# Eight quarter-sized casting weight loads for four halves, and a newly searched unit order, in a fused linear-attention and feed-forward kernel

## The chip, the cores and the metric

The kernel runs on one core of one Trainium2 chip. The metric is device time in microseconds (us). Every comparison below sets a kernel beside the kernel before, run in turn with it on the same chip in the same rounds. A ratio is the mean time of one kernel's fast runs over the mean of the other's fast runs of the same rounds, so it is not quite the ratio of the medians that are quoted; its 95% interval follows in brackets. For a single core a run counts as slow when it is over 1.5% above the fastest of the same kernel. Two changed kernels were mostly run in different rounds, so they are compared through their ratios to the kernel before. The time covers a little more than the profiled span: 195.0 us beside a span of 192.9 us in the profiled run of the kernel before.

## The reference, cut to what matters

```python
# q, k, v, alpha: (4 batches, 8 heads, 768 steps, 48), float32
for t in range(S):
    state = alpha[:, :, t, :, None] * state + einsum('bhd,bhe->bhde', k[:, :, t], v[:, :, t])
    y[:, :, t] = einsum('bhd,bhde->bhe', q[:, :, t], state)
x = y.transpose(0, 2, 1, 3).reshape(3072, 384)
h = x @ w_in                # (384, 2048)
out = (h * cos(h)) @ w_out  # (2048, 384)
```

## The kernel before

The sequence is cut into 24 chunks of 128 steps. Each chunk needs four loads (alpha, k, q, v, with rows of 192 bytes), the logarithm of alpha, cumulative sums on TensorE, exponentials, two scalings, transposes of q and k, scores, a state update and the attention output. Its output then goes through the two layers. All of it is written as small **units**, and one string gives their order; each engine runs its own units in that order. A unit waits for its inputs, and everything behind it on the same engine waits with it. So the order is the schedule.

```python
units = {
    "a": load_a, "k": load(k_t, k), "q": load(q_t, q), "v": load(v_t, v), "w": load_w,   # w from GpSimd, the rest on the SP queue
    "l": ..., "C": ..., "E": ...,        # logarithm (ScalarE), cumulative sums (TensorE), exponentials (ScalarE) of a pair of chunks
    "K": scale_k, "R": lambda j: scale_q(nc.gpsimd, j), "O": lambda j: scale_q(nc.vector, j),
    "P": cast_v, "M": decay,             # GpSimd
    "T": transposes, "t": ev_transposes, # on TensorE, copied out by VectorE
    "D": dma_transposes,                 # or as one DMA on the SP queue
    "S": state, "A": scores, "Q": outputs_two, ...
    "F"/"H": first layer, "f"/"h": Sin, "p"/"g": gate, "V": second layer (a quarter), "o": store, "x": warmup,
}
for u in ORDER.split():
    units[u[0]](int(u[1:]))

def load_w(i):                           # float32 in memory, bfloat16 on the chip: a casting DMA, issued by GpSimd
    n = NF // 2
    if i < 2:
        f = slice(i * n * C, (i + 1) * n * C)
        nc.gpsimd.dma_start(out=w1[:, :, f], in_=moe_w_in[:, f].rearrange("(k p) f -> p k f", p=C))
    else: ...                            # the halves of w_out

def dma_transposes(j):
    nc.sync.dma_start_transpose(qkT[j % 4]..., kqb[j % 4]...)
```

The loads, the stores and the DMA transposes share one queue, SP. A DMA transpose whose input is not ready holds every load behind it; in the trace of the kernel before, such waits add up to 20.6 us.

## Time and profile before

| | before |
|---|---|
| median of 3 runs | 195.2 us (195.06 to 195.44) |
| profiled span, granted clock | 192.9 us, 1.00 |
| busy: TensorE, VectorE, ScalarE, GpSimd | 95%, 61%, 62%, 42% |
| DMA row | 8 or 9 tenths from about 5 to 150 us |
| TensorE waits after 46 us | 1.8 us in all |

A busy share says how long an engine had work, not whether it was the bound. Here two rows are full, TensorE's and the DMA row, and TensorE's includes 17 us of warm-up matmuls that compute nothing. The chain of waits and the list of TensorE's waits tell more: TensorE waits for data until 43 us (the **ramp**) and is fed afterwards (the **rest**). The lines are in the prediction.

### The profile page before, as it was taken

Reading aid. Unit: us, or ns where it says so; the run is one execution under the profiler, and the core shown is the slowest. Engines: PE = TensorE matmul, PEld = TensorE weight load, DVE = VectorE, ACT = ScalarE, POOL = GpSimd, SP = SyncE. Lnnn points to the kernel's source line nnn. Section 1 sums busy time; section 2 is a strip of 40 time slices with the busy share of each in tenths; the row PEclk is TensorE's granted clock in tenths of the full one; section 3 lists DMA queues with packets and bytes.
Section 4 is the critical chain, followed back from the end, with each engine's and each line's share of the span. In section 5 each row is a group of like instructions: output and inputs, shape, how many; then the busy total and the mean of one; then the engine's idle time right before and its main releaser. Section 6 shows DMA issues by size and latency. Waiting matters only on the chain.

```text
span 192.9 us, 4781 instructions
## 1 busy us (share of the span) xinstructions
PE 182.5 (95%) x1990; PEld 131.8 (68%) x1994; DVE 117.7 (61%) x138; ACT 120.1 (62%) x133; POOL 81.6 (42%) x128
## 2 busy tenths in 40 slices
PE   7997889989999999997999998999999999999993
PEld 2444468957688687685777685786786786876861
DVE  5025784844847928829828438748758578596450
ACT  2540344744768668947739567789999982361632
POOL 3317950055294655571190656271239761030000
PEclk9999999999999999999999999999999999999999
DMA  6999999999989999999989999999998762200112
GB/s 127 188 187 188 146 190 188 184 196 194 190 192 176 205 233 207 188 168 196 268 162 192 175 214 218 175 227 205 149 217 158 135 152 34 85 0 3 41 41 82
DMA packets 123092, 31.23 MB, mean 162 GB/s; under 512 B 117184, under 2 KB 122304, under 8 KB 123072
## 3 DMA queue, kind: packets, MB, share of 16 engines
q1 hardware_dynamic: 120192, 27.80, 85.0%
q0 software_dynamic: 2880, 3.15, 10.1%
q8 instruction: 15, 0.25, 0.5%
q14 instruction: 5, 0.04, 0.1%
HBM read 25.17 MB, written 4.72 MB: 155 GB/s over the span
## 4 chain that ended last, share of the span: by engine, by line
PE 66%; DMA 13%; SPq 6%; ACT 4%; issue 4%; DVE 3%; POOL 2%; ACTq 0%; DVEq 0%
PE one L362 31%; PE two L341 21%; DMA w<-in_moe_w_out_dram 10%; PE two L303 6%; SPq L158 5%; PE two L243 3%; DVE g_sb L352 3%; DMA v_sb<-in_v_dram 2%; ACT c_sb L347 2%; PE two L191 2%; SPq L161 2%; ACT L347 1%; PE one L257 1%; POOL w L167 1%; PE two L193 1%
## 5 line engine op out<-in xcount | busy, mean ns | idle before, releaser
L352 DVE TENSOR_TENSOR g_sb<-two,c_sb 128x1024 bf16<-128x1024 f32 x48 | 58.0, 1221 | 27.7 <-ACT c_sb L347 27.2
L362 PE MATMUL one<-w,g_sb 128*128 128x384 bf16 x384 | 69.5, 327 | 1.4 <-DVE g_sb L352 0.8
L341 PE MATMUL two<-xT,w 128*128 128x256 bf16 (+1 forms) x624 | 68.4, 264 | 1.0 <-DVE g_sb L352 1.0
L347 ACT ACTIVATE c_sb<-two,halfpi 128x1024 bf16<-128x1024 f32 x48 | 52.6, 1113 | 19.5 <-PE two L341 19.0
L341 PEld LDWEIGHTS <-w 128*128 128x128 bf16 x624 | 56.7, 98 | 9.7 <-issue 1.1
L362 PEld LDWEIGHTS <-g_sb 128*128 128x128 bf16 x384 | 35.3, 98 | 24.0 <-DVE g_sb L352 1.7
L206 POOL TENSOR_TENSOR kqb<-k_sb,icp 128x384 bf16<-128x384 f32 x24 | 23.9, 997 | 20.5 <-DMA k_sb<-in_k_dram 12.6
L262 POOL TENSOR_TENSOR ub<-sc,Em 128x384 bf16<-128x384 f32 x20 | 16.6, 829 | 33.1 <-DVE sc L272 31.8
L248 DVE TENSOR_TENSOR A_sb<-two,mask_f 128x1024 bf16<-128x1024 f32 x24 | 28.5, 1217 | 2.6 <-PE two L243 2.6
L212 POOL TENSOR_TENSOR kqb<-q_sb,cp 128x384 bf16<-128x384 f32 x22 | 21.9, 998 | 9.4 <-DMA q_sb<-in_q_dram 5.7
L366 ACT ACTIVATE o_sb<-one 128x384 f32<-128x384 f32 x24 | 11.7, 492 | 15.5 <-PE one L362 15.5
L347 ACT ACT_TABLE_LOAD x11 | 14.1, 1283 | 9.9 <-PE two L341 6.2
L216 POOL CAST vpb<-v_sb 128x384 bf16<-128x384 f32 x24 | 12.0, 504 | 17.2 <-DMA v_sb<-in_v_dram 9.3
L375 PE MATMUL one<-warm 128*128 128x512 bf16 x62 | 17.1, 418 | 2.2 <-DVE warm L102 1.2
L185 ACT ACTIVATE lnab<-a_sb 128x768 bf16<-128x768 f32 (+1 forms) x13 | 10.3, 794 | 12.5 <-DMA a_sb<-in_alpha_dram 12.4
L201 ACT ACTIVATE icp<-two 128x768 f32<-128x768 f32 (+1 forms) x13 | 9.9, 761 | 11.8 <-PE two L193 9.0
L272 DVE TENSOR_TENSOR sc<-one,ub 128x384 f32<-128x384 f32 x20 | 11.0, 552 | 8.2 <-PE one L257 7.9
L321 DVE CAST xT<-two 128x768 bf16<-128x768 f32 x11 | 10.5, 958 | 8.4 <-PE two L303 8.4
L179 ACT ACT_TABLE_LOAD x11 | 14.1, 1283 | 0.9 <-PEq L404 0.7
L303 PE MATMUL two<-A_sb,vpb 128*64 128x128 bf16 x264 | 13.2, 220 | 0.1
L303 PEld LDWEIGHTS <-vpb 128*64 128x64 bf16 x288 | 12.8, 110 | 0.5 <-issue 0.3
L375 PEld LDWEIGHTS <-warm 128*128 128x128 bf16 x66 | 6.4, 104 | 9.6 <-issue 3.6
(42 smaller groups left out, 114.1 us busy)
## 6 DMA issues: line engine op xcount, KB each, us to landing
k_sb<-in_k_dram SPq DMA_DIRECT2D x24, 192.0 KB, 4.6
a_sb<-in_alpha_dram SPq DMA_DIRECT2D x24, 192.0 KB, 4.3
v_sb<-in_v_dram SPq DMA_DIRECT2D x24, 192.0 KB, 4.4
q_sb<-in_q_dram SPq DMA_DIRECT2D x24, 192.0 KB, 4.2
out_dram<-o_sb SPq DMA_DIRECT2D x24, 192.0 KB, 3.7
w<-in_moe_w_in_dram POOLq DMA_DIRECT2D x2, 768.0 KB, 10.0
w<-in_moe_w_out_dram POOLq DMA_DIRECT2D x2, 768.0 KB, 17.7
qkT<-kqb SPq DMA_TRANSPOSE x16, 3.8
```

What stands on the lines that cost most here:

```text
L179: nc.scalar.preload_act_table_set("natural_log_exp_and_others")
L206: nc.gpsimd.tensor_tensor(out=kqb[j % 4][:, 0, :, 0:D], in0=k_t[j % 6], in1=icp_t[j // 2 % 3][:, j % 2].rearrange("s (h d) -> s h d", h=H) ...
L212: eng.tensor_tensor(out=kqb[j % 4][:, 1, :, 0:D], in0=q_t[j % 6], in1=cp.rearrange("s (h d) -> s h d", h=H), op=ALU.mult)
L216: nc.gpsimd.tensor_copy(out=vpb[j % 4][:, :, 0:D], in_=v_t[j % 6])
L248: nc.vector.tensor_tensor(out=A_t[j % 4].rearrange("s (h t) -> s h t", h=H), in0=two[("A", j)].rearrange("s (h t) -> s h t", h=H), in1=mas ...
L262: eng.tensor_tensor(out=ub[j % 3][:, :, 0:96].rearrange("r p (a e) -> r p a e", a=2), in0=src.rearrange("r p (a e) -> r p a e", a=2), in1= ...
L303: nc.tensor.matmul(t[64 * half : 64 * half + 64, kt * C : (kt + 1) * C], lhsT, rhs, start=start, stop=stop, skip_group_check=True)
L341: nc.tensor.matmul(t[:, m * n : (m + 1) * n], w1[:, kk, f * C : (f + 1) * C], x_t[g % 3][:, kk, bs].rearrange("r b t -> r (b t)"), start=( ...
L347: nc.scalar.activation(out=c_s.take((name, i)), in_=two[(name, i)], func=AF.Sin, bias=halfpi, scale=1.0)
L352: nc.vector.tensor_tensor(out=g_t[g % 3][:, fs, bs], in0=shaped(two[(name, i)], name), in1=shaped(c_s[(name, i)], name), op=ALU.mult)
L362: nc.tensor.matmul(one[("o", j)][:, 0:DM], g_t[j // 2 % 3][:, f, j % 2], w2[:, f], start=(f == 0), stop=(f == NF - 1))
L375: nc.tensor.matmul((one.free or two.free)[0][:, 0:512], warm[:, 0:C], warm, start=True, stop=True)
```

## The change

Its intent: the weights are to come in smaller steps, so that the first layer waits for fewer of them at a time. The first unit F0 still needs both quarters of the first half of w_in, 768 KB (in bfloat16); only the later, smaller units H can do with 384 KB. The order of all units was searched anew, by a local search over a recalibrated timing model. In the new order eight more of the q and k scalings run on VectorE, chunks 5, 6 and 7 are transposed by DMA instead of TensorE, and the activation table is switched 20 times instead of 22.

```diff
 ORDER = """
-k1 a0 a3 a1 k0 v1 q0 a2 q2 i0 x12 c0 v3 d0 k2 M0 i1 x7 c1 k3 K0 d1 q1 K1 q3 P1 O0 x13 T0 v0 l1 t0
...
-C3 m4 b4 o2 V12 E3 m5 V13 k7 S5 Q2 l4 u5 M7 M6 o0 R6 C4 z2 a11 M5 K6 V14 E4 H10 v7 b5 q8 T6 P6 k8
-H8 t6 h10 R7 q11 S6 a10 V15 h8 g10 K7 H9 q9 e3 u6 g8 M9 T7 k9 M8 h9 H11 t7 k10 P7 g9 V16 h11 v8 R8
...
+a2 w1 a1 a0 a3 i0 l1 i1 v0 k0 q3 q0 k3 P0 x32 C1 c0 d0 B0 w0 x6 S0 R0 M0 c1 v1 d1 E1 x1 T0 t0 u0
...
+k6 q7 k7 e2 E3 V12 o0 q6 v6 V13 M6 R7 K7 K6 l4 m5 Q2 C4 z2 E4 S5 V14 H10 P6 H8 a11 v7 D7 P7 M7 h10
+O6 u5 H9 S6 V15 D6 g10 h8 H11 h9 e3 g8 u6 V16 S7 A7 g9 u7 h11 A6 V17 m7 a10 m6 o2 k8 q8 k9 a13 v9
... (27 lines each, all replaced)
@@ load_w @@
-        n = NF // 2
-        if i < 2:
+        n = NF // 4
+        if i < 4:
...
-            i -= 2
+            i -= 4
@@ scale_k takes the engine; "B" is new @@
-        "K": scale_k,
+        "K": lambda j: scale_k(nc.gpsimd, j), "B": lambda j: scale_k(nc.vector, j),
```

More of the change, by code (lines that the diff above doesn't have):

```diff
@@ L17 @@
 ORDER = """
-k1 a0 a3 a1 k0 v1 q0 a2 q2 i0 x12 c0 v3 d0 k2 M0 i1 x7 c1 k3 K0 d1 q1 K1 q3 P1 O0 x13 T0 v0 l1 t0
-a5 x2 C1 E1 a4 v2 K2 q5 R2 K3 k5 x15 T2 O1 t2 T1 k4 A0 t1 q4 P0 x1 A1 w0 S1 S0 a6 u0 w1 u1 l2 M1
-m0 R3 x8 C2 w2 m1 T3 E2 M2 Y0 w3 t3 A2 y0 P2 Y1 m2 b1 S2 A3 M3 P3 u2 M4 m3 b2 Q1 x6 F0 z1 y1 S3 f0
-F2 p0 f2 x2 F3 p2 F1 f3 H6 p3 f1 H4 p1 h6 u3 V4 h4 g6 b3 V5 V0 g4 V1 v4 H5 a7 V2 h5 v5 R5 V3 g5 V6
-a8 e0 K5 V7 a9 H7 K4 e1 q6 R4 T5 h7 V8 t5 k6 V9 g7 T4 v9 P4 V10 t4 v6 V11 l3 S4 e2 A4 q7 u4 A5 P5
@@ L23 @@
-C3 m4 b4 o2 V12 E3 m5 V13 k7 S5 Q2 l4 u5 M7 M6 o0 R6 C4 z2 a11 M5 K6 V14 E4 H10 v7 b5 q8 T6 P6 k8
-H8 t6 h10 R7 q11 S6 a10 V15 h8 g10 K7 H9 q9 e3 u6 g8 M9 T7 k9 M8 h9 H11 t7 k10 P7 g9 V16 h11 v8 R8
-S7 A6 u7 A7 o1 V17 m6 b7 V20 a13 m7 V21 V18 a12 l5 g11 Q3 o3 R9 C5 z3 v10 K8 V19 E5 H12 K9 D8 e4
-R11 H14 D9 M10 P8 H13 h12 K10 o4 q10 k11 g12 S8 h13 V22 v11 V23 u8 h14 q12 g13 H15 b8 e5 P10 k12
-g14 V28 M11 k13 h15 P9 S10 V29 a15 g15 V30 a14 A8 R10 l6 A9 m8 V31 v12 K11 C6 e7 m9 E6 S9 D10 P11
-Q4 u9 b9 D11 V24 z4 R12 V25 u10 v13 H18 K12 v14 b10 H16 D12 h18 H19 q15 g18 h16 o5 P12 S11 g16 h19
@@ L29 @@
-H17 M12 v15 u11 o7 V26 g19 h17 V27 a16 P13 V32 g17 e6 M13 A10 q13 A11 m10 S12 V33 o6 l7 V34 a17
-m11 C7 k14 Q5 E7 a18 u12 A12 z5 P15 V36 R15 V37 m12 K13 V38 H22 R13 M15 H20 D13 b11 h22 P14 H21
-q19 g22 K14 h20 q17 q14 V35 g20 v16 h21 V39 k15 q21 e8 H23 g21 e9 o9 V40 h23 S13 V41 u13 R14 g23
-A13 V44 b13 l8 D14 V45 m13 V46 K15 q20 V47 v17 C8 D15 Q6 E8 P16 q16 V42 z6 a19 e11 V43 M16 R17 k17
-H24 o8 q18 P17 k16 M14 S14 a21 h24 H25 u14 b14 e10 g24 S15 h25 o10 H26 R16 k18 g25 V48 h26 K17 H27
-u15 g26 D17 b15 V52 h27 V53 a20 K16 v18 A15 A14 a23 m15 V49 D16 l9 V50 m14 V54 v19 C9 g27 Q7 E9
@@ L35 @@
-K18 V55 z7 V51 R18 e13 H28 o13 e12 R19 a22 o12 S16 M18 D18 S17 u16 H30 h28 b16 o11 g28 H29 q23 P19
-h30 k19 P18 v22 M17 u17 V60 q22 h29 g30 V56 H31 g29 l10 A17 A16 m17 V61 V62 K19 m16 h31 V57 D19
-V58 g31 C10 k20 Q8 E10 V59 z8 V63 R20 e14 H32 o14 e15 b17 k21 o15 K20 S18 k23 S19 u18 H34 h32 v21
-R21 u19 D20 M19 g32 H33 b19 h34 v20 K21 v23 V68 g34 h33 k22 M20 V64 D21 H35 g33 P21 l11 A18 A19
-m18 V69 V70 P20 m19 M21 h35 V65 V66 g35 C11 Q9 E11 P22 V67 z9 P23 K23 V71 e16 H36 o16 e17 M22 R23
-o17 S20 R22 D23 H38 u20 h36 b20 H37 g36 h38 K22 M23 S21 D22 g38 h37 V76 H39 u21 g37 b21 V72 h39
@@ L41 @@
-A21 A20 m21 V77 V78 m20 V73 V74 g39 A22 Q10 V75 z10 V79 e18 m22 H40 o18 e19 o19 S23 h40 S22 H42
-u22 b22 g40 H41 h42 u23 V80 b23 g42 h41 H43 g41 A23 h43 V84 m23 V81 g43 V82 Q11 V83 z11 V85 e20
-H45 o20 V86 h45 H44 g45 H47 h44 H46 g44 h47 V87 g47 h46 V88 e21 V89 g46 o21 V92 V93 V90 V91 V94
-e22 V95 o22 e23 o23
+a2 w1 a1 a0 a3 i0 l1 i1 v0 k0 q3 q0 k3 P0 x32 C1 c0 d0 B0 w0 x6 S0 R0 M0 c1 v1 d1 E1 x1 T0 t0 u0
+B3 x3 A0 k1 m0 R3 M3 P1 M1 K1 M2 q1 x5 T3 a5 a4 t3 k2 Y0 y0 w3 x1 A3 q2 S1 F0 O1 l2 T1 C2 m3 u1 R2
@@ new lines @@
+E2 t1 B2 A1 m1 v2 x3 T2 t2 w2 w4 P2 b1 Y1 A2 y1 S2 v3 m2 F2 P3 f0 u2 b2 S3 p0 w5 w6 f2 Q1 k4 q5 k5
+p2 M4 w7 u3 z1 x1 F1 f1 F3 V4 V0 H5 f3 h5 p1 p3 g5 v4 q4 a6 a7 H6 H4 M5 b3 K5 V5 H7 K4 P4 h6 h4 h7
+V1 g6 g4 O5 V6 O4 g7 V7 V2 V3 e1 V8 e0 D5 V9 T4 t4 V10 V11 S4 a9 v5 a8 u4 o1 b4 l3 A4 m4 P5 A5 C3
+k6 q7 k7 e2 E3 V12 o0 q6 v6 V13 M6 R7 K7 K6 l4 m5 Q2 C4 z2 E4 S5 V14 H10 P6 H8 a11 v7 D7 P7 M7 h10
+O6 u5 H9 S6 V15 D6 g10 h8 H11 h9 e3 g8 u6 V16 S7 A7 g9 u7 h11 A6 V17 m7 a10 m6 o2 k8 q8 k9 a13 v9
+q9 v8 l5 V20 b5 V21 V18 C5 Q3 g11 V22 V19 z3 M8 B9 R8 M9 K8 R9 b7 P8 H12 H14 E5 h12 e4 H13 V23 g12
@@ new lines @@
+h14 g14 h13 e5 H15 g13 S8 V28 u8 o3 k11 a12 v10 h15 b8 P9 D9 D8 V29 A9 A8 V30 g15 m8 k10 q10 o5
+v11 k12 o4 q11 a14 k13 a16 m9 V31 l6 e7 C6 P10 K10 S9 S10 E6 u9 Q4 V24 O10 z4 V25 P11 b9 O11 u10
+K11 M10 M11 K12 b10 M12 H18 M13 K13 S11 H16 h18 h16 H19 g18 h19 H17 q12 D10 q13 u11 D11 R12 g16
+g19 h17 V26 a15 V27 e6 D12 o7 R13 V32 A11 A10 V36 l7 g17 k14 D13 v12 V37 V38 C7 V39 m11 m10 o6 b11
+k15 P12 a17 Q5 k17 v13 v14 q15 E7 q14 A12 A13 V33 z5 m12 m13 V34 H22 V35 H20 e9 l8 h22 e8 h20 P13
+K15 K14 P14 R15 R14 g22 S13 H21 S12 H23 h21 g20 u12 Q6 V44 g21 u13 z6 h23 C8 g23 a18 o9 v15 q17 o8
@@ new lines @@
+k16 k19 q16 a19 v16 D15 V45 H24 H25 S14 V46 E8 h24 b13 H26 V47 u14 g24 V40 h25 M14 M16 b14 R17 K17
+P15 g25 h26 e11 K16 V41 D14 A14 P16 g26 l9 M15 v17 A15 m14 m15 V42 V43 S15 C9 v18 q18 o11 k18 q19
+D17 Q7 e10 z7 u15 E9 H27 H30 S16 H28 P18 K18 R18 R16 a20 q21 o10 h27 V52 h28 D16 g27 b15 h30 R19
+a23 u16 g28 g30 V53 H29 V54 V48 V55 A16 A17 K19 b16 P17 M18 M17 k23 a21 k20 v20 v22 V49 V50 D19
+h29 g29 l10 e13 m17 m16 C10 V51 S17 Q8 z8 o13 H31 e12 E10 S18 H33 h31 u17 u18 g31 V56 V60 v21 o12
+D18 k22 a22 k21 v19 P21 P20 P19 K21 q22 q20 q23 h33 g33 A18 A19 V57 V58 H32 l11 h32 m18 m19 g32
@@ new lines @@
+V59 e14 Q9 V61 S19 C11 H34 V62 u19 z9 E11 h34 g34 V63 H35 H39 V64 e15 h35 h39 g35 g39 b17 H36 V65
+M19 K20 b19 R21 V66 R20 R22 R23 K22 P22 M20 K23 V67 o14 h36 e16 H38 S20 D21 D22 o15 g36 u20 h38
+M21 M22 b20 H37 S21 V68 V69 h37 V70 u21 D23 D20 g38 g37 V72 V71 A21 A20 A23 V73 e17 m20 m21 V74
+V75 Q10 m23 z10 A22 V76 e18 o16 S22 V77 H40 v23 V78 h40 V79 H41 e19 P23 M23 o17 b21 h41 m22 u22
+g40 b22 Q11 H42 S23 o18 z11 V84 H43 h42 h43 u23 g42 g41 g43 V80 H44 V81 V82 h44 H46 V85 V83 H45
+V86 e20 h46 h45 g44 V88 V87 e21 g45 g46 o19 o20 o21 H47 h47 V89 V92 g47 V90 V93 V94 V91 e22 o22
@@ L45 @@
+V95 e23 b23 o23
 """
@@ L203, in exps, with scale_k @@
         two.give(("c", j))
-    def scale_k(j):
-        nc.gpsimd.tensor_tensor(out=kqb[j % 4][:, 0, :, 0:D], in0=k_t[j % 6],
+    def scale_k(eng, j):
+        eng.tensor_tensor(out=kqb[j % 4][:, 0, :, 0:D], in0=k_t[j % 6],
                                 in1=icp_t[j // 2 % 3][:, j % 2].rearrange("s (h d) -> s h d", h=H),
@@ L379 @@
         "l": lambda g: ln(2 * g, 2), "C": lambda g: cums(2 * g, 2), "E": lambda g: exps(2 * g, 2),
-        "K": scale_k, "R": lambda j: scale_q(nc.gpsimd, j), "O": lambda j: scale_q(nc.vector, j),
+        "K": lambda j: scale_k(nc.gpsimd, j), "B": lambda j: scale_k(nc.vector, j), "R": lambda j: scale_q(nc.gpsimd, j), "O": lambda j: scale_q(nc.vector, j),
         "P": cast_v, "M": decay,
```

## The prediction

> **What bounds the kernel now.** I began with the page: its first part (engine shares) and the row of DMA busy tenths. TensorE's matmul row is busy nearly all the time, and the DMA row stands at 9 until about 155 us, so both are suspects and neither share says which one a change would move.
>
> ```profile
> PE 182.5 (95%) x1990; PEld 131.8 (68%) x1994; DVE 117.7 (61%) x138; ACT 120.1 (62%) x133; POOL 81.6 (42%) x128
> ...
> q0 software_dynamic: 2880, 3.15, 10.1%
> ```
>
> The 95% is not all work. The busy time by stretches, restricted to the warm-up line L375 (columns: stretch, its length, PE busy and count, PEld busy and count, clock, DMA share, GB/s), shows 17 us of dummy matmuls, all before 42.8 us:
>
> ```profile
> 0.00:28.50 28.50, 15.44 (x56) 5.88 (x60) 1.00 1.20 170
> 28.50:42.80 14.30, 1.62 (x6) 0.55 (x6) 1.00 1.25 194
> ```
>
> The waits of PE after 42.8 us are these three and no others, 2.3 us in all:
>
> ```profile
> PE two L341 <- DVE g_sb L352: 1.0, 1, 1.0
> PE one L362 <- DVE g_sb L352: 0.8, 1, 0.8
> PE one L362 <- DMA w<-in_moe_w_out_dram: 0.5, 1, 0.5
> ```
>
> So there are two regimes: a ramp of 43 us, in which TensorE waits or warms itself, and 147 us in which it is fed. The chain that ended last names what sets the ramp (start, length, what):
>
> ```profile
> 13.86 4.62 DMA v_sb<-in_v_dram
> ...
> 18.53 0.50 POOL vpb L216
> 19.04 1.65 POOL w L167 x2
> ...
> 22.92 19.84 DMA w<-in_moe_w_out_dram
> ...
> 42.80 2.76 PE one L362 x16
> ```
>
> The weight DMAs stand behind a cast of v in GpSimd's program order, so they are issued only at 19 to 23 us, and the last half lands at 42.76. The timeline of the SP queue shows what they do to the other loads meanwhile:
>
> ```profile
> 18.13 2.35 SPq L158 DMA_DIRECT2D q_sb<-in_q_dram  x1
> 20.53 10.01 SPq L158 DMA_DIRECT2D k_sb<-in_k_dram  x2
> 30.59 5.38 SPq L158 DMA_DIRECT2D q_sb<-in_q_dram  x1
> ```
>
> A load issue takes about 1.0 us before the weights and some 5 us beside them.
>
> **A ledger of TensorE.** From the chain I take the spacing of each unit: a first-layer unit 1.31 us (48 equivalents), a quarter of the second layer 0.65 (96), a score unit 0.275 (24), state 0.17 (24), cumulative sums 0.26 per chunk (24), attention outputs 1.24 per pair, TensorE transposes 0.45 each (8). Sum: 62.9 + 62.5 + 6.6 + 4.1 + 6.2 + 14 + 3.6 = about 160 us of useful work, against an end of matmuls at 189.65. By 42.8 us about 19.6 us of it is done (7.9 of attention, four F units, three H units, four second-layer quarters). So 23 us of the roughly 30 us that are not work lie in the ramp, the rest in the three waits and small spacings. The tail after the last matmul is 3.25 us.
>
> **What the Trainium skill says.** (1) "DMA: Bandwidth & Descriptors", section "Issuing engines are not separate DMA queues": DMAs from all queues run on the same 16 engines and interleave. The trace agrees: the SP loads above slow down by five. So splitting transfers adds no bandwidth; only their order can help. (2) The same page, "Queues, rings and completion order": each DMA engine takes turns between queues at packet granularity. I read from the trace that the weights win these turns: 22 us held 19.5 us of weight time (10.1% of 192.9), near 85%. (3) "SBUF — State Buffer", section "Who interferes with whom": a VectorE instruction with two SBUF inputs contends with a GpSimd instruction that reads SBUF. The q scalings on VectorE agree, the second ran beside a GpSimd scaling:
>
> ```profile
> 10.15 0.67 DVE L212 TENSOR_TENSOR kqb<-q_sb,cp 128x384 bf16<-128x384 f32 x1 [6.61 <-DMA q_sb<-in_q_dram]
> ...
> 16.46 1.25 DVE L212 TENSOR_TENSOR kqb<-q_sb,cp 128x384 bf16<-128x384 f32 x1 [4.45 <-DMA q_sb<-in_q_dram]
> ```
>
> **The change, part by part.** I counted the units of both orders.
>
> *Weight DMAs, 4 to 8.* The issues cost GpSimd 0.79 to 0.94 us whether for 384 or 1024 rows, so I take them as fixed: eight cost about 7 us against 3.6, which is +3.4 us on an engine at 42%. DMA time stays at 19.5 us, about 2.44 per quarter; halving w_in's rows may add a little. The landings of the halves were 7.9 us (the first) to 19.8 us (the last) after issue. A half takes about 5.2 us in company, so the start-up is about 2.7 us and a lone quarter should land 5.3 us after its issue.
>
> *Ramp.* The first 15 loads land at about 2.7 + 1.05n us (second alpha at 4.8, eighth load at 11.1, fifteenth at 18.5). The new order issues the second quarter of w_in at once (about 2.3 us) and v0 as fifth load, then the first quarter behind its cast. Both quarters are in by about 16 to 17 us. The first F unit then waits for the attention chain alone: q0 about 13.5 to 14, its scaling, transposes, scores, mask, output, eviction, each by its row: F0 at 20 to 22 us instead of 29.6. That is the attractive part. But F1 and F3 need the other quarters of w_in. In GpSimd's order the last of these stands behind the scaling of q2, the 16th load: 2.7 + 16.8 + 4.9 for two quarters = 24.4, and some 2 us later because the third quarter goes in front, so 26.5. Scaling to 27.5, landing at 27.5 + 5.3 = 33 us; the first quarter of w_out follows near 35.5. Before, F3 began at 32.9 us, with the same work done. By DMA bytes alone: eight quarters (19.5 us) plus about 20 loads (21 us) plus 2.7 is 43 us, as before. By the new order about 20 to 21.4 us of useful work should then be done instead of 19.6. I take a **gain of 0.9 us** in the ramp; up to 3 us is open, for the new order carries 14 fewer warm-up matmuls (52 against 66), and 14 x 0.216 us = 3.0.
>
> *Transposes.* Five chunks go through TensorE instead of eight: 3 x 0.45 = **1.35 us off TensorE** in the full part, and 3 x 0.69 us off VectorE. In exchange come three DMA transposes on a DMA row that is full until 155 us: 1.2 to 1.9 us each on the SP queue.
>
> *GpSimd to VectorE.* Four k and four more q scalings leave GpSimd (8 x 1.0 us) for VectorE (8 x 0.67 to 1.25, 5 to 10 us). VectorE rises from 117.7 to about 123 us, GpSimd falls from 81.6 to about 77. Neither is near the bound, so directly nothing.
>
> *Table loads.* The switches of the activation table fall from 22 to 20, 2 x 1.28 us off ScalarE. Two of the three PE waits above follow such a load and Sin, then the gate. I credit **half of the 2.3 us, 1.2 us**.
>
> Sum: 195.2 - 0.9 - 1.35 - 1.2 = 191.7 us.
>
> **Rivals.** *A: the ramp opens fully.* The new order's fill of warm-ups is right, the q2 load is not delayed and the quarters of w_in land by 29 us: 3 us more, 188 to 189 us. For it: F0 is free much earlier, and the first 32 warm-ups (to about 10.3 us) fit the landing of alpha that I get. Against: the DMA byte count, which no order of transfers changes. *B: the DMA row becomes the bound.* The chunks sent through DMA transposes now include 5; that transpose stands behind two dozen loads, so near 48 us its issue and about 52 its landing, while its scores are due at about 50. Late in the kernel the last transposes issue at 154.6 to 157 us before; the new order asks for the scores of chunk 23 some 10 us sooner, and 32 us of TensorE work follow. Three more transposes, 4 us of traffic, could hold it by 2 to 4 us: 194 to 197 us. Against: the SP queue waits about 20 us for GpSimd in front of transposes, which the lighter GpSimd shortens. *C: nothing moves*, since the transfer that ends the ramp lands at 43 us either way and old gaps come back elsewhere: 194 to 195 us.
>
> **Range and chances.** The centre is the sum above. A and B pull by some 3 us either way and C by 3 upward, so 8 in 10 is 188.2 to 195.6 us. The 2% line is 191.3; with the centre just above it and A and an order that was searched for on its side, I give faster 0.44, within 2% 0.53, slower 0.03.
>
> **What would show it.** Right: F0's matmuls at 20 to 22 us but the second-layer line starting no sooner than 34 us; the last weight landing at 41 to 44 us; DVE L212 and L206 rows with means between 0.67 and 1.25 us; PE waits after the ramp under 2 us in all. Wrong: a second-layer start by 31 us (then A), or PE waits of several us for transposes or scalings around 50 or 158 us (then B), or a clock below 1.00 after a long early idle of TensorE, which I do not expect.

## The result, and the profile after

| | before | after |
|---|---|---|
| median, same rounds | 195.26 us (195.06 to 195.44, 4 runs) | 201.09 us (200.5 to 202.31, 4 runs) |
| ratio | | 1.0307 [1.0258, 1.0356] |
| profiled span, granted clock | 192.9 us, 1.00 | 198.9 us, 0.99 |

The change made the kernel **3% slower**. First, from the page, TensorE's share and the queue of the weights:

```profile
PE 179.0 (90%) x1954; PEld 130.3 (65%) x1956; DVE 120.1 (60%) x143; ACT 116.8 (59%) x131; POOL 77.2 (39%) x124
...
q0 software_dynamic: 3712, 3.15, 10.3%
```

TensorE does 3.5 us less in a span that is 6 us longer. The weights take 832 more packets for the same bytes and about the same DMA time. The warm-up line by stretches (length, matmuls busy and count, weight loads busy and count, clock, DMA share, GB/s):

```profile
0.00:28.50 28.50, 13.46 (x49) 5.05 (x51) 1.00 1.02 173
28.50:46.40 17.90, 0.39 (x1) 0.10 (x1) 0.91 1.16 177
```

The warm-ups fell by 3.3 us, as the order says. The clock in the second stretch is 0.91: TensorE ran slowed within the ramp, which it did not before. Split finer, over all of TensorE's work (stretch, length, busy time of TensorE, weight loads, VectorE, ScalarE and GpSimd, clock, DMA share, GB/s):

```profile
26.00:29.00 3.00, 1.15 (x22) 1.05 (x24) 0.69 (x1) 2.18 (x2) 2.19 (x3) 0.88 1.26 196
29.00:32.00 3.00, 3.00 (x40) 2.63 (x37) 2.52 (x4) 0.00 (x0) 2.27 (x5) 0.55 1.10 156
```

TensorE was busy 1.15 us of 3, and in the next 3 us the clock was 0.55. A first-layer unit of one chunk, F0, takes 1.50 us from its first matmul to its last at full clock (at 20.25 us); F2 took 2.24 us in the slowed stretch. The Trainium skill, "TensorE: Matmul & The Clock Gate", section "Part 1: The HAM clock gate", says that the clock falls to half after an idle window of about 3.4 us. The trace agrees in kind: the longest single wait before it was 2.33 us, but almost 2 of 3 us were idle. From 36 to 189 us the clock is 1.00 in this trace, and in those of runs 7, 8, 16 and 17 below, so what is lost after the ramp is not lost by the clock.

The chain of waits shows what set the ramp after (start, length, what):

```profile
19.54 7.19 DMA q_sb<-in_q_dram
...
26.81 0.98 POOL kqb L212
...
28.55 0.78 POOL w L171
...
34.29 12.07 DMA w<-in_moe_w_out_dram
...
46.41 3.41 PE one L362 x20
```

The last weights stand behind the scaling of q2 in GpSimd's order, as the prediction says, but the last quarter needs 12 us from issue to landing and ends the ramp at 46.4 instead of 42.8 us. In the timeline of the SP queue two loads stand beside these weights, and then the queue does nothing until 46 us:

```profile
30.53 7.21 SPq L161 DMA_DIRECT2D a_sb<-in_alpha_dram  x2
46.00 1.34 SPq L236 DMA_TRANSPOSE qkT<-kqb  x1
```

The waits of the SP queue name the holder, the scaling of q5 on VectorE (times and longest follow the sum):

```profile
SPq L236 <- DVE kqb L212: 8.1, 1, 8.1
```

Most of the loss comes after the ramp. TensorE's waits from 46 us on are these five and two more of 0.4 and 0.2 us, 7.7 us in all, against 1.8 us before:

```profile
PE two L243 <- DMA qkT<-kqb: 1.9, 3, 0.7
PE one L257 <- POOL vpb L216: 1.9, 1, 1.9
PE two L191 <- ACT lnab L185: 1.3, 1, 1.3
PE two L341 <- DVE g_sb L352: 1.3, 3, 0.5
PE two L243 <- DVE g_sb L352: 0.7, 1, 0.7
```

The first is a DMA transpose, the second a cast of v, the third a logarithm of alpha. The cast itself takes half a microsecond; in the page's groups its idle time shows for what it waits, first before, then after:

```profile
L216 POOL CAST vpb<-v_sb 128x384 bf16<-128x384 f32 x24 | 12.0, 504 | 17.2 <-DMA v_sb<-in_v_dram 9.3
```

```profile
L216 POOL CAST vpb<-v_sb 128x384 bf16<-128x384 f32 x24 | 12.0, 503 | 41.3 <-DMA v_sb<-in_v_dram 38.7
```

GpSimd waited 38.7 us for loads of v, four times as long. The logarithm shows the same for alpha, 21.3 us against 12.4. And the chain that ended last ran mainly along TensorE before, and runs along loads and their issues after (before, then after):

```profile
PE 66%; DMA 13%; SPq 6%; ACT 4%; issue 4%; DVE 3%; POOL 2%; ACTq 0%; DVEq 0%
```

```profile
PE 40%; SPq 22%; DMA 20%; POOL 8%; issue 3%; ACT 3%; DVE 2%; POOLq 0%; ACTq 0%; DVEq 0%
```

**The ledger after.** With the prediction's unit times, some 21.4 us of useful work are done at 46.41 us, so 25.0 us are lost there, against 23.2 us before (42.8 less 19.6): 1.8 us more. From there to the last matmul, at 195.26 us, 148.85 us pass for some 137.2 us of work, 11.6 us lost. Before, 146.85 us passed (to 189.65 us) for 140.4 us of work, 6.4 us lost. So the rest loses 5.2 us more. Three transposes fewer on TensorE give 1.35 us back. The sum, 5.6 us, is the distance between the two ends, and the times differ by 5.8 us. How it is split is an estimate, since the unit times are the prediction's.

### The profile page after: what moved, and what is told of

Same layout as the page of the kernel before. It is cut to its first block, busy times and chain, and to the rows that moved or that the text cites. A ratio compares the mean times of both kernels' runs of the same rounds, so it can differ in the third digit from the quotient of the medians.

```text
span 198.9 us, 4708 instructions
## 1 busy us (share of the span) xinstructions
PE 179.0 (90%) x1954; PEld 130.3 (65%) x1956; DVE 120.1 (60%) x143; ACT 116.8 (59%) x131; POOL 77.2 (39%) x124
## 4 chain that ended last, share of the span: by engine, by line
PE 40%; SPq 22%; DMA 20%; POOL 8%; issue 3%; ACT 3%; DVE 2%; POOLq 0%; ACTq 0%; DVEq 0%
PE one L362 17%; PE two L341 15%; SPq L158 13%; DMA w<-in_moe_w_out_dram 6%; DMA q_sb<-in_q_dram 6%; SPq L161 4%; SPq L236 4%; DMA k_sb<-in_k_dram 4%; PE two L303 4%; POOL ub L262 3%; DMA a_sb<-in_alpha_dram 2%; DMA v_sb<-in_v_dram 2%; POOL kqb L212 2%; ACT c_sb L347 2%; SPq L370 1%
## 5 line engine op out<-in xcount | busy, mean ns | idle before, releaser
L341 PE MATMUL two<-xT,w 128*128 128x256 bf16 (+1 forms) x624 | 69.8, 266 | 1.3 <-DVE g_sb L352 1.3
L341 PEld LDWEIGHTS <-w 128*128 128x128 bf16 x624 | 57.3, 99 | 10.3 <-issue 1.8
L216 POOL CAST vpb<-v_sb 128x384 bf16<-128x384 f32 x24 | 12.0, 503 | 41.3 <-DMA v_sb<-in_v_dram 38.7
L212 POOL TENSOR_TENSOR kqb<-q_sb,cp 128x384 bf16<-128x384 f32 x18 | 17.7, 997 | 18.4 <-DMA q_sb<-in_q_dram 17.1
L185 ACT ACTIVATE lnab<-a_sb 128x768 bf16<-128x768 f32 (+1 forms) x13 | 10.2, 793 | 21.4 <-DMA a_sb<-in_alpha_dram 21.3
L206 POOL TENSOR_TENSOR kqb<-k_sb,icp 128x384 bf16<-128x384 f32 x20 | 19.8, 996 | 3.4 <-DMA k_sb<-in_k_dram 2.4
L375 PE MATMUL one<-warm 128*128 128x512 bf16 x50 | 13.8, 417 | 2.4 <-DVE warm L102 1.2
L303 PE MATMUL two<-qkT,ub 128*64 128x128 bf16 x152 | 11.4, 222 | 0.0
```

Source lines behind the costliest of these rows:

```text
L206: eng.tensor_tensor(out=kqb[j % 4][:, 0, :, 0:D], in0=k_t[j % 6], in1=icp_t[j // 2 % 3][:, j % 2].rearrange("s (h d) -> s h d", h=H), op=A ...
L212: eng.tensor_tensor(out=kqb[j % 4][:, 1, :, 0:D], in0=q_t[j % 6], in1=cp.rearrange("s (h d) -> s h d", h=H), op=ALU.mult)
L303: nc.tensor.matmul(t[64 * half : 64 * half + 64, kt * C : (kt + 1) * C], lhsT, rhs, start=start, stop=stop, skip_group_check=True)
L341: nc.tensor.matmul(t[:, m * n : (m + 1) * n], w1[:, kk, f * C : (f + 1) * C], x_t[g % 3][:, kk, bs].rearrange("r b t -> r (b t)"), start=( ...
L375: nc.tensor.matmul((one.free or two.free)[0][:, 0:512], warm[:, 0:C], warm, start=True, stop=True)
```

## The experiments

The theories: **Hold**: the scaling of q5 on VectorE stands 8.1 us in front of the first early DMA transpose, and all loads behind it come late. **Early transposes**: transposes of chunks 5 to 7 in the SP queue delay the loads behind them on a full DMA row. **Ramp**: the quarters' issues on GpSimd, or their landing, cost the time. **Order of the loads**: the new order asks for later chunks too soon and issues their loads too late, whatever else it does. The edits name units; "..." marks the unchanged order around them. Where lines of code are numbered one less than in the kernels above (L157 for L158), an experiment's order took a line less.

### 1. The hold taken away (a_O5early)

```diff
 (after) ... M4 w7
+O5
 u3 z1 ... g6 g4
-O5
 V6 O4 ...
```

> The changed kernel with one unit moved: the VectorE scaling of q5 goes ahead of the eviction of state 3 instead of behind seven gates, so that the DMA transpose of chunk 5 can issue at about 38 us instead of 46.0 and no longer holds the loads behind it in the SP queue for 8.1 us. Theory 1 (that hold made the four to five loads of deficit that starve the middle): 3 to 5 us off, 196 to 198 us, loads issued by 60 us back to 39 or 40 instead of 35. Theory 2 (the traffic of three more DMA transposes does it): within 1 us of 201.1. Theory 3 (the late weights of the ramp do it): within 1 us of 201.1.

Measured: 200.75 us, ratio 1.0256 [1.0213, 1.0299]. The hold was gone, but the two alpha loads in front of the transpose now took 8.05 us to issue beside the weights, so the transpose went out at 43.06 us instead of 46.00, and by 60 us only 36 loads were out, against 35 in the changed kernel and 40 before. About 1 us of 6 came back. This run alone tests the hold weakly; run 8 below has no such hold and loses nearly as much, so the hold is not the main cause.

### 2. The early transposes back on TensorE (a_T567)

```diff
 (after) ... e0
-D5
 V9 T4 t4 V10 V11
+T5 t5
 S4 ... a11 v7
-D7
 ... S6 V15
-D6
 ... u6
+T7 t7
 V16
+T6 t6
 S7 ...
```

> The changed kernel with chunks 5, 6 and 7 transposed on TensorE again, as before the change: no hold in the SP queue and three DMA transposes fewer, but 1.35 us more of TensorE work. Theory 1: no better than the run with q5 scaled early, 196.5 to 199 us. Theory 2: some 3 to 4 us faster than that run, 193 to 195 us. Theory 3: 201 to 202.5 us.

Measured: 202.71 us, ratio 1.0367 [1.0341, 1.0393], no better. A new hold of 7.6 us had come up, near 70 us: the next transposes in the queue waited for the k scaling of chunk 9, which the new order puts on VectorE. Its trace also has the clock at 0.52 from 69 to 72 us. So this run did not test the theory cleanly, and runs 13, 16 and 17 came from it.

### 3. Quarters alone (b_quarters)

```diff
 (before, each half issued as two quarters in place)
-        n = NF // 2
+        n = NF // 4
...
-w0 ... w1 ... w2 ... w3
+w0 w1 ... w2 w3 ... w4 w5 ... w6 w7
```

> The kernel before with each half-sized weight DMA cut into two quarters issued in its place; nothing else. If the quarters themselves cost (issue time on GpSimd 3.2 us more, twice the rows for w_in), 1 to 3 us slower, 196 to 198 us. If only the order costs, 194.5 to 196 us.

Measured: 197.88 us, ratio 1.0152 [1.0104, 1.0199]. The profiled run was the fastest of the four, 196.5 us. Its timeline of GpSimd shows what moved:

```profile
19.09 3.25 POOL L166 DMA_DIRECT2D w<-in_moe_w_in_dram  x4
22.36 0.22 POOL L219 TENSOR_TENSOR Em<-cp,m 128x8 f32<-128x8 f32 x1
```

The two halves took 1.7 us at this place before. A quarter's issue costs GpSimd as much as a half's (3.25/4 = 0.81 us), so everything behind moved: the second decay of the state from 26.58 to 28.73 us and the first first-layer unit from 29.62 to 31.72 us. The clock read 0.56 from 21 to 24 us in this trace; the trace of run 10 reads the same there, at 195.43 us, so the clock is not what costs here. Splitting alone, in the old order, cost about 2.7 us (197.88 less 195.18). That it does so through the later units of GpSimd is read from this trace and was not tested apart.

### 4. Three DMA transposes added to the old order (b_3moreD)

```diff
 (before; X is a DMA transpose of the same chunk into a spare tile)
 ... K9 D8
+X8
 ... D10
+X10
 ... D12
+X12
```

> The kernel before with three redundant DMA transposes (chunks 8, 10 and 12 once more, into a spare tile that nobody reads), each right behind the transpose of the same chunk; the result stays right. It adds the traffic and nothing else. Theory 2 (traffic): 3 to 5 us slower, 198 to 200 us. Theory 1: under 1.5 us slower, 195 to 196.7 us.

Measured: 196.65 us, ratio 1.0068 [1.0034, 1.0101], so 1.3 us (0.0068 x 195.2). Three transposes on the full DMA row are not free, but they are far from the loss.

### 5. Halves in the new order (a_halves)

```diff
 (after, with halves)
-a2 w1 ... B0 w0 ... y0 w3 ... t2 w2 w4 ... p0 w5 w6 ... M4 w7
+a2 w0 ... B0    ... y0 w1 ... t2 w2    ... p0 w3    ... M4
```

> The changed kernel with four half-sized weight DMAs again, each where the earlier (for the last two: the first-needed) of its quarters stood; four GpSimd issues of about 0.78 us fewer. In the order of before the quarters cost 2.7 us through GpSimd's program order. If they cost the same way here, 2 to 3 us faster than the changed kernel, 198 to 199 us. If their cost depends on the old order only (here the new order was searched around them), within 1 us of 201.1; slower, 202 to 204, if the quarters help the first F unit start.

Measured: 203.01 us (200.59 to 205.0); on the two fast runs of four 1.0294 [1.0253, 1.0335]. The quarters are neither the cure nor the main harm in the order that was searched for them.

### 6. Weights earlier in the new order (a_wearly)

```diff
 (after) ... y0 w3
+w2 w4
 ... T2 t2
-w2 w4
```

> The changed kernel with the third w_in quarter and the first w_out quarter issued right behind the quarter before them, ahead of the scaling of q2 that waits until 26.7 us for its load. If that wait sets the end of the ramp, the w_out matmuls start at 34 to 35 us instead of 37.6 and 1.5 to 3 us come off (198 to 199.5). If the ramp is set by the sum of bytes, q2 is only pushed back further and the time is 200.5 to 203 us.

Measured: 204.92 us, ratio 1.0468 [1.04, 1.0535]. It got worse. Its profile shows the scaling of q2 start at 29.1 instead of 26.8 us and the first second-layer unit at 40.48 instead of 37.58 us, which I take as a hint only. The time itself says that weights that leave GpSimd sooner do not open the ramp here. That they take the DMA row from the loads that TensorE waits for is the likely reason; run 15 shows it.

### 7 and 8. Each part of the order with the other's rest

Run 7 has the new order up to the third pair of cumulative sums (about 50 us), then the old one; run 8 the old one, with halves, then the new one.

```diff
 (7: hyb_newramp_oldrest)   after[.. C3] + before[rest, units already done left out]
 (8: hyb_oldramp_newrest)   before[.. C3] + after[rest, units already done left out]
```

> The new order up to the cumulative sums of group 3 (about 53 us), then all remaining units in the old order, with chunks 6 and 7 through TensorE. The ledger of the two traces gives about 1.8 us lost in the ramp and 5.2 in the rest, 1.35 gained from transposes. If the rest loses because of its own order and its transposes, this is 196.5 to 198 us. If it loses because the ramp leaves the loads behind, it stays at 200 to 202 us.

> The old order with halves up to the same point, then the rest in the new order (two transposes more than before). If the rest loses because of its own order and traffic, 197 to 200 us. If the loss comes out of the ramp, 193 to 196 us.

Measured: run 7, 197.63 us, ratio 1.0117 [1.0061, 1.0173]; run 8, 201.02 us, ratio 1.0285 [1.0239, 1.0331]. So the **rest** carries most of it: the new rest behind the old ramp costs 5.6 us, the new ramp before the old rest 2.3 us (each ratio less one, times 195.4). Together that is more than the change's 6 us, so the two overlap; presumably a later ramp gives the late loads of the rest some time back. Run 7 holds its SP queue for 8.1 us like the changed kernel, at the same scaling, and after 46 us it has only the two old waits of 1.0 and 0.8 us, and two of 0.4 and 0.2 us: the hold by itself does little harm to the old rest. In run 8 no transpose waits over 4.1 us, and nearly the whole loss is there.

### 9 and 10. The v loads left out (a_noV, b_noV)

```diff
 (after and before; the scores and states from chunk 6 on use old data)
-"v": load(v_t, v)
+"v": lambda j: load(v_t, v)(j) if j < 6 else None
```

> The changed kernel without the loads of v for chunks 6 to 23 (the casts read old tiles; the result is wrong on purpose). 18 of 96 loads are gone, some 19 us of DMA time, all of it after the ramp. If the middle is starved by DMA (theory 2 in its wide form: loads come late because the transfers ahead of them fill the queue), the PE waits for lnab, vpb and qkT after 46 us shrink under 1.5 us together and 4 to 6 us come off: 195 to 197 us. If engine order is what starves it, 199.5 to 201 us.

> The kernel before with the same loads left out (wrong on purpose). Its PE waits only 1.8 us after the ramp and none of it for a load, so under either theory 194 to 195.4 us.

Measured: the new order without 18 loads 195.19 us, ratio 1.0003 [0.9953, 1.0054]; the old order without them 195.24 us, ratio 0.9996 [0.9975, 1.0017]. Leaving them out takes the **whole** difference away in the new order, and gives the old order nothing. TensorE's waits after 46 us in run 9, with one more of 0.5 us:

```profile
PE two L341 <- DVE g_sb L352: 1.2, 2, 1.0
PE two L243 <- DVE g_sb L352: 0.7, 1, 0.7
PE two L243 <- DMA qkT<-kqb: 0.6, 1, 0.6
```

The waits for v and for alpha are both gone, though only the loads of v are, and the waits for transposes fell from 1.9 to 0.6 us: the other transfers came earlier on the freed row. So the loss is late transfers, and the old order had time to spare for them.

### 11. The scalings back on GpSimd (a_BOundone)

```diff
 (after)
-B0 B3 B2 O5 O4 O6 B9 O10 O11
+K0 K3 K2 R5 R4 R6 K9 R10 R11
```

> The changed kernel with its new VectorE scalings of k and q (chunks 0, 2, 3, 9 and 4, 5, 6, 10, 11) on GpSimd again, at the same place of the order. If moving them to VectorE cost time (scalings stuck behind gates, transposes stuck behind scalings in the SP queue), 197 to 200 us. If the move relieved GpSimd as meant, slower: 202 to 205 us. Within 1 us of 201.1 if it does not matter.

Measured: 202.74 us, ratio 1.0369 [1.0338, 1.0399]. Undoing this part makes it no faster. The move to VectorE is not what costs.

### 12. The old order with its ramp rearranged by hand (b_better)

```diff
 (before, from Q1 to K4; x6, x2 and the later H7 h7 g7 left out)
-Q1 x6 F0 z1 y1 S3 f0 F2 p0 f2 x2 F3 p2 F1 f3 H6 p3 f1 H4 p1 h6 u3 V4 h4 g6 b3 V5 V0 g4 V1 v4 H5 a7 V2 h5 v5 R5 V3 g5 V6 ...
+Q1 y1 F0 z1 S3 f0 F2 p0 f2 H4 p2 h4 H5 g4 h5 F3 g5 f3 F1 p3 f1 H6 p1 h6 u3 H7 g6 h7 V4 b3 V5 g7 V0 V1 v4 a7 V2 v5 R5 V3 V6 ...
```

> The kernel before with the ramp alone rearranged: two groups of warm-ups out, the y1 eviction ahead of z1, H4 and H5 (which need only the first half of w_in) ahead of F3 and F1, H7 ahead of the first second-layer quarter. The weights land as before; 1.3 us more of work is done by 42.8 us and the wait of 0.5 us there goes. Expected 193.2 to 194.2 us; 195 or more if the rearranged units wait for something else.

Measured: **194.33 us**, ratio 0.9948 [0.9933, 0.9963], a little faster than both kernels. Two first-layer units now run where warm-ups and waits stood, and the halves are kept. What it meets next is the last half of w_out, for which TensorE waits 1.4 us. The ramp of this kernel ends with the landing of the weights, as the prediction's count would have it.

### 13. Old ramp, new rest, without early transposes (oldramp_newrest_T67)

```diff
 (run 8) ... v7
-D7
 ... V15
-D6
 ... u6
+T7 t7
 V16
+T6 t6
 S7 ...
```

> The old ramp and the new rest again (201.0 us before), with chunks 6 and 7 through TensorE, as in the kernel before, so that the number of DMA transposes is 16 in both. If the early transposes are what puts the loads behind (their traffic, and the wait for the scalings in the SP queue, at 50 to 62 us), 3 to 5 us faster, 196 to 198 us. If the order of the loads in the SP queue is, within 1.5 us of 201.

Measured: 201.72 us, ratio 1.0302 [1.0244, 1.036]. Again a hold of 5.7 us for the k scaling of chunk 9 had come up, so it was repeated without it in run 16.

### 14. Two early transposes in the old order (b_D67)

```diff
 (before; chunks 6 and 7 by DMA, right behind the load of v7, and four loads behind them)
-q8 T6 ... k8 ... t6 ... q11 ... a10 ... T7 ... t7
+D7 D6 q8 k8 q11 a10
```

> The counterpart: the kernel before with chunks 6 and 7 through DMA transposes, set into the SP queue where the new order has them, right behind the load of v7. If the early transposes are the cause, 3 to 5 us slower, 198 to 200 us, with loads issued by 60 us down from 41 to 36 or 37. If the order of the loads is, under 2 us slower.

Measured: 198.82 us, ratio 1.0183 [1.0162, 1.0204]. So early transposes, with four loads moved behind them, cost 3.6 us in the *old* order. TensorE waits 2.0 us for one of them, and right after that wait the clock reads 0.59 (66 to 69 us) and 0.84 (69 to 72 us), where it is 1.00 in the trace before. That can be up to 1.7 us of the 3.6 (an estimate: 0.41 and 0.16 of 3 us each). In the old order the swap of TensorE transposes for DMA transposes is a bad trade, though TensorE is freed of some 0.9 us (2 x 0.45). It is not yet the cause of the loss, as runs 16 and 17 show.

### 15. Four second-layer units moved into gaps, and a weight load earlier (b_better2)

```diff
 (run 12) ... q4
+w0
 P0 x1 A1
-w0
 ... V26 V27 put in front of H17, V47 behind Q6, V43 in front of e10
```

> The rearranged ramp of the faster version (194.33 us) and three small moves more: the first weight half issues ahead of the cast of v0 (0.9 us earlier, in an idle gap of GpSimd), two second-layer quarters go ahead of H17 and one behind H25, into the two TensorE gaps of 1.0 and 0.8 us. 1.5 to 2.5 us faster than that version, 192 to 193 us; 194 or more if the gaps only move.

Measured: 197.41 us, ratio 1.012 [1.0081, 1.0158], slower than run 12. One wait took it, the first of its list of TensorE waits:

```profile
PE one L257 <- POOL vpb L216: 4.9, 1, 4.9
```

The first weights now issue at 17.30 instead of 18.98 us, right behind the load of v2 (16.99 us), and this load lands late: its cast runs at 29.32 instead of 23.83 us. Earlier weights took the row from a load that TensorE waits for. After 46 us, however, the waits had fallen to 0.8 us in all, so the four moved units did their part.

### 16 and 17. No early transposes, and the scaling of chunk 9 back on GpSimd (oldramp_newrest_T67_K9, a_T567_K9)

```diff
 (16: run 13; 17: run 2)
-B9
+K9
```

> The order before up to the third pair of cumulative sums (with the weights in halves), then the new order, with chunks 6 and 7 transposed on TensorE (as in the earlier run of that kind, 201.7 us), and now also the k scaling of chunk 9 moved back from VectorE to GpSimd. In the earlier run a DMA transpose stood 5.7 us at the head of the SP queue for that scaling. Theory 'held queue' (early DMA transposes and the holds in front of them keep back the loads behind them, and nothing else in the rest of the order costs much): with both gone the time falls to 196 to 198.5 us. Theory 'order of the loads' (the new order is short of loads because of where they stand among stores, computations and each other, whatever the transposes do): it stays at 200 to 202 us.

> The changed kernel with chunks 5, 6 and 7 transposed on TensorE (202.7 us in the earlier run, where a DMA transpose stood 7.6 us for the k scaling of chunk 9 on VectorE) and that scaling moved back to GpSimd. Theory 'held queue': without the three early DMA transposes and without the hold, 197 to 199.5 us, since only the ramp's loss of about 2 us stays. Theory 'order of the loads': 200.5 to 203 us.

Measured: run 16, 201.17 us, ratio 1.0276 [1.0229, 1.0324], against 1.0285 for run 8; run 17, 201.42 us, ratio 1.0311 [1.0268, 1.0353], against 1.0307 for the change itself. Nothing came back. But the queue did not run freely either: where a transpose had stood for the scaling of chunk 9 in runs 13 and 2 (5.7 and 7.6 us), the store of chunk 5 now stood for its result. From the waits of the SP queue between 66 and 84 us, first run 16, then run 17:

```profile
SPq L370 <- ACT o_sb L366: 3.7, 1, 3.7
```

```profile
SPq L370 <- ACT o_sb L366: 6.8, 1, 6.8
```

So **the loss does not need the early transposes, nor the two holds named so far**; that stops in the queue cost nothing is not shown. In the changed kernel itself no wait of this queue is over 2.0 us between 46 and 146 us. What TensorE no longer waits for DMA transposes, it waits elsewhere; in run 16 the idle of TensorE from 46 to 180 us is 6.4 us, against 7.7 us after and 2.0 us before (each stretch less its busy time).

What stayed is the place of the loads. The timelines of the SP queue from 85 to 103 us show it, first before:

```profile
86.57 1.26 SPq L158 DMA_DIRECT2D v_sb<-in_v_dram  x2
87.95 1.65 SPq L236 DMA_TRANSPOSE qkT<-kqb  x1
...
99.22 1.24 SPq L236 DMA_TRANSPOSE qkT<-kqb  x1
```

Then after the change:

```profile
90.11 1.24 SPq L236 DMA_TRANSPOSE qkT<-kqb  x1
...
92.09 1.40 SPq L236 DMA_TRANSPOSE qkT<-kqb  x1
...
94.70 1.59 SPq L236 DMA_TRANSPOSE qkT<-kqb  x1
96.35 0.57 SPq L158 DMA_DIRECT2D v_sb<-in_v_dram  x1
...
100.28 3.05 SPq L158 DMA_DIRECT2D v_sb<-in_v_dram  x2
```

Then run 16:

```profile
95.03 0.57 SPq L158 DMA_DIRECT2D v_sb<-in_v_dram  x1
...
99.17 2.22 SPq L158 DMA_DIRECT2D v_sb<-in_v_dram  x2
```

The pair of loads of v13 and v14 goes out at 86.6, 100.3 and 99.2 us. I matched each issue to its unit by counting along the queue, and added up TensorE's work in front of the unit that needs it, with the prediction's unit times. That is how much work of the order precedes the need:

| data, and the unit that needs it | issue: before, after, run 16 | TensorE work ahead of the need: before, after, run 16 |
|---|---|---|
| v13, state of chunk 13 | 86.6, 100.3, 99.2 us | 79.1, 74.6, 75.9 us |
| alpha of chunks 20 and 21, cumulative sums | 121.7, 130.5, 128.3 us | 109.0, 101.6, 102.9 us |
| alpha of chunks 22 and 23, cumulative sums | 127.8, 141.1, 138.8 us | 122.0, 114.1, 115.5 us |

The new order needs these data 4.5 to 8 us of work sooner and asks for them 9 to 14 us later. The waits of the changed kernel for a cast of v near 105 us and for a logarithm of alpha between 120 and 140 us fall on the first two rows; the third met no wait. Not every chunk lost on both sides: the state of chunk 12 is needed 9.6 us of work later than before, with its v issued 14.8 us later. In the three rows 16 to 21 us of spare time are gone, of which the later end of the ramp returns 3.6 us in the changed kernel. It is not that the queue moves less: by 100 us it had issued 79 transfers in both kernels (before 65 loads, 6 transposes, 8 stores; after 62, 9, 8), and 77 in run 16 (63, 6, 8). But others stand in front of these. Counted in the orders, 65 transfers go ahead of the load of v13 before, 79 after and 76 in run 16; ahead of the later load of the alpha pairs it is 100, 108 and 105, and 106, 118 and 115. So each place further back came to about 1 us of delay in the changed kernel (14 places, 13.7 us; 8, 8.8 us; 12, 13.3 us). That this order of loads against needs costs the time fits run 9 and these two runs; I did not run the new order with just these loads put forward, so it is argued from the traces and not shown alone.

### 18. The rearranged ramp with the gaps filled (b_better3)

```diff
 (run 12) ... g16 h19
+V26 V27
 H17 ...                  (V47 behind Q6, V43 in front of e10, as in run 15; w0 stays)
```

> The rearranged ramp of the earlier run that beat both kernels (194.3 us), with four second-layer quarters moved to where TensorE waited 1.0 and 0.8 us for a gate, but without the earlier weight issue that cost 4.9 us in the second try. Theory 'two regimes' (ramp bound by bytes, then TensorE fed): the moved quarters take some 1.2 us of waits away and nothing else changes, 192.8 to 194.0 us. Rival 'a saturated row gives it back': the fuller TensorE meets a late load instead, 194.3 to 195.3 us.

Measured: **193.64 us** (193.06 to 193.68), ratio 0.9911 [0.9897, 0.9924]: faster than both kernels, by 1.7 us against the kernel before (0.0089 x 195.28) and some 7.5 us against the change (201.09 less 193.64, in other rounds). It is within 2% of the kernel before all the same. Of TensorE's waits after 46 us these were left:

```profile
PE one L362 <- DVE g_sb L352: 0.6, 2, 0.5
PE one L257 <- POOL vpb L216: 0.2, 1, 0.2
```

## Why the prediction was wrong

It said 191.7 us, with 0.03 for slower; it came to 201.09. Point by point:

- **The start of the ramp was right.** F0 ran from 20.25 us (predicted 20 to 22). The scaling of q2 ended at 27.8 us (predicted to 27.5) and held the second part of the weights.
- **The gain of 0.9 us in the ramp was wrong.** The step that failed is to carry "a lone quarter should land 5.3 us after its issue" over to w_out. For w_in it nearly held: the page's median is 6.0 us, and the unit that needs its last quarter ran from 33.98 us (landing predicted at 33). But the second layer started at 37.58 us on a quarter of w_out predicted near 35.5, and those four, issued from 28.5 to 34.3 us, took 9.7 us (median) and 12.07 us (the last). Nor does the count of 43 us by bytes hold when the row has slack: its share from 0 to 28.5 us fell from 1.20 to 1.02. So the last weight came at 46.4 us, outside the predicted 41 to 44, and the ramp lost 1.8 us by the ledger (2.3 us in run 7).
- **3.4 us of issues on "an engine at 42%", not charged in the sum: wrong in kind.** The issue cost was sized right, at 0.81 us each. But the issues stand in series in GpSimd's order in front of a cast and a decay that TensorE awaits. Run 3 puts about 2.7 us on the split in the old order. The engine's average share over 193 us says nothing of its load from 19 to 27 us.
- **The DMA transposes were sized but not charged.** The prediction took 1.35 us off for TensorE, and left the 1.2 to 1.9 us of each on the SP queue out of its sum. Runs 4 and 14 show a price of 1.3 and 3.6 us in the old order (of the latter up to 1.7 us by the clock). TensorE's busy time without warm-ups fell only from 165.4 to 165.2 us, presumably because the slowed clock took the rest.
- **The 1.2 us off the last gaps was wrong, and this is the largest miss.** The table switches did fall, but the waits after 46 us rose from 1.8 to 7.7 us; by the ledger the rest lost 5.2 us more, where the prediction had it gain. The step that failed is that TensorE stays fed after 43 us: the prediction took the new rest to be fed because the old one was. It never set the issue time of each load against its need in the new order, though it noted that chunk 23 is asked for some 10 us sooner and used that for the last transposes only.
- **Rival B had the right place and too small a size.** It gave 194 to 197 us for the DMA row as the bound, by transposes. Transfers were the bound (run 9), but by all loads, and without the early transposes the loss is the same (runs 16 and 17, which have the stop at a store instead). The wait around 48 us that it named for chunk 5 happened, as a hold, and runs 1 and 8 show that it was not what counted.
- **The clock** was not expected below 1.00; it was 0.55 for 3 us, some 0.7 us on one first-layer unit (2.24 less 1.50), in a ramp whose end the last weights set.
- **"Directly nothing" for the scalings on VectorE was right**: run 11, which undoes them, was no faster.
- The odds leaned on an order "that was searched for". The search's model had no more proof than the prediction, and 0.03 for slower was far too sure.

Open: which of the loads would have to move for the new rest to work, and whether it would then beat the old one; and how much of the loss in runs 16 and 17 comes from the stop at the store of chunk 5, which took the place of the hold in runs 13 and 2.

## What to carry to other kernels

Where a transfer row is full, judge a new order by the time between each load's issue and its need, not by shares: here up to 21 us of that spare time went, and a run without 18 of the loads had no loss at all. Count an engine's issue instructions where they stand in its program, not against its average. A cheap rearrangement of the old schedule at a place that the trace names (193.64 us) did more than a full new search.

## What the Trainium skill lacked or had wrong

- "DMA: Bandwidth & Descriptors", section "Issuing engines are not separate DMA queues", calls the sequencer's time to initiate a DMA "usually small relative to the DMA itself". That is so here, but it does not make it free: a casting DMA from GpSimd took some 0.8 to 0.9 us to issue, whether half or quarter, and four more of them cost about 2.7 us (run 3), probably because the units behind them in GpSimd's order start later. The page does agree that all queues share the row: a pair of alpha loads took 7.2 us to issue beside the weights.
- The same page, section "Anatomy of one DMA — SWDGE (gpsimd) path", gives about 2.0 us plus bytes over 436 GB/s for one transfer. That is 2.9 us for the 384 KB that a quarter writes (an estimate from the page), while the runs show medians of 6.0 and 9.7 us and 12.07 us for the last, in company. No page says how much of the row such transfers and loads with 192-byte rows get when they meet.
- "TensorE: Matmul & The Clock Gate" speaks of an idle window of about 3.4 us. Here the clock read 0.55 over 3 us with no single wait above 2.33 us before it, after 3 us of which 1.15 us were busy; run 14 shows the like after a wait of 2.0 us. So the idle time need not be one unbroken wait of that length.
- No page says what a DMA transpose costs the loads behind it on a full row: three added ones cost 1.3 us (run 4), two early ones, with four loads behind them, 3.6 us (run 14, up to 1.7 us of it by the clock).
